# Attention ahead of a mixture of experts: value products of two query halves in two column groups, two pairs behind their scores

## The chip, the cores and the metric

The kernel runs on one NeuronCore of a Trainium2 chip. The metric is the device time of one execution in microseconds (us). The kernel before took 699.36 us (median of three runs, 698.83 to 700.39). The profile shown here is of one execution of 699.8 us.

## The reference, cut to what matters

```
q, k, v: [8, 8, 576, 64] float32                  # batch, heads, positions, head size
scores = q @ k.T / 8
heads 0-3: keep keys with 0 <= pos_q - pos_k < 32                # "local"
heads 4-7: keep keys with pos_k <= pos_q and equal pos % 32      # "strided"
attn = softmax(scores);  x[b, s, h*64:(h+1)*64] = attn @ v
logits = x @ w_gate;  local_gate = sigmoid(x @ w_local)
for s in order: e = argmax(logits[s]) if s == 0 or local_gate[s] < 0.5 else the e of s-1
out[b, s] = softmax(logits[s])[e] * relu(x[b, s] @ w1[e]) @ w2[e]     # 512 -> 1024 -> 512
```

All arithmetic is float32. On TensorE one float32 matmul appears in the trace as two passes, each with its own weight load: six matmuls give twelve records.

## The kernel before, in words

The kernel has two stages. The first is attention with the gate, some 7 to 160 us of the profile. The second is the experts: tokens are sorted by expert into tiles of 128, gathered from the array `xd` in HBM, multiplied by the expert's two matrices, and scattered to the output (L944, L1067, L1088, L1092). The change is in the first stage and in the routing that sorts the tokens.

**A step.** Attention goes by pairs of heads: 8 batches of 4 pairs, two local and two strided, so 32 pairs, one in each step of the loop at L520. Queries are cut into blocks: a local head has six blocks of 96 queries against 128 keys; a strided head is first reordered so that equal residues stand together, and has three blocks of 108 and two of 126. A pair is worked in two units (`Unit`, g = 0 and 1): three blocks each, or three and two. Each step has, on TensorE:

- **scores** (L361): keys are the stationary operand, queries move, 64 rows of contraction. The two heads of the pair lie in the two row halves of the array. ScalarE takes the exponential out of PSUM into the tile `e` (L365), VectorE multiplies it by the mask (L368).
- **values** (L408) of the pair one step behind: `e` of one block is stationary (96, 108 or 126 columns, all 128 rows of contraction or the block's), and the values with a column of ones move. The moving slice is not 65 columns wide but as wide as the block: `values` takes the neighbouring head's columns too and overwrites them with the next product. VectorE adds 1e-9 to the sums (L416), takes the reciprocal (L418) and scales the rows into the x tile `xl` or `xs` (L419).
- **transposes of x** (L445) of the pair two steps behind; ScalarE copies them into `xT` (L449, L452).
- once per batch, **gates** (L462: four products of 32 columns side by side in four column groups) and **choices** (L478), the logits and VectorE's small steps on them.

The x tiles are stored to `xd` by `store_x`, one transfer for a local group (L427), five for a strided one (L431). There is one buffer each of `xl` and `xs`. Loads of q, k and v of the next batch are issued at the first pair of each group (`load`), on the same SyncE queue as the stores. That queue issues in program order: behind a store that waits for VectorE, the next load waits too.

**Order.** The tile framework schedules instructions and keeps each engine's queue in order; `tc.issue_after(x)` forces an instruction behind x on its engine. Before the change only a few places use it.

**Routing.** `route` is a generator that does the bookkeeping of the sort; it runs once for the first three batches (`first`, inside the attention loop, one piece per step), and once for all eight during the first experts. In its pieces stand long VectorE instructions over 576 positions (L580, L587, L668 to L685) and small matmuls. `PIECES` (L69) says at which steps the weights of the first two experts are loaded, eight loads of 1 MB; L228 says where gathers start. At the end of attention the first expert's hidden products fill waits (`filling`, L1067).

Of the kernel before, what the change touches and what calls it, by code (L numbers as in the profile page):

```python
# [19 lines left out]
P = 128  # L20
# [16 lines left out]
SX = 7 * SP  # L37
KW = STRIDE + S
# [3 lines left out]
GC = 32  # L42

# [12 lines left out]
BE = 3  # L56
# [12 lines left out]
PIECES = (7, 9, 11, 13, 15, 16, 17, 18)  # L69
# [3 lines left out]
SUM_LO, SUM_HI = 0.1, 1.0e30  # L73
# [17 lines left out]
class Unit:  # L91


    def __init__(self, b, pair, g):
        self.b, self.pair, self.g = b, pair, g
        self.grp, self.i2 = divmod(pair, 2)
        self.local = self.grp == 0
        self.n = (b * PAIRS + pair) * 2 + g
        if self.local:
            self.w, self.kb, self.m, self.t0 = LQ, LK, 3, 3 * g  # L100
            self.cols = [t * LQ for t in range(3 * g, 3 * g + 3)]
        else:
            self.t0, self.m = (0, 3) if g == 0 else (3, 2)
            self.w = self.kb = SBLK[self.t0][1] * SP
            self.cols = [SBLK[t][0] * SP for t in range(self.t0, self.t0 + self.m)]
# [15 lines left out]
def attention_then_scomoe(ctx: ExitStack, tc: tile.TileContext, q, k, vl, vs, wg, w1, w2, out):  # L121
# [7 lines left out]
    sums = once.tile([P, B * PAIRS * 2, 2, 3], F32, name="sums")  # L129
    nc.gpsimd.memset(sums, 1.0)  # L130
# [3 lines left out]
    passes(tc, False, q, k, vl, vs, wg, w1, w2, views, xd, c, sums, bad)  # L134
    again = nc.values_load(bad[0:1, 0:1], min_val=0, max_val=P,
                           skip_runtime_bounds_check_because="a count of partitions")
    with tc.If(again > 0):

        seen = once.tile([1, 2], F32, name="seen")
        for i, v in enumerate(views):  # L140
            nc.gpsimd.dma_start(out=seen[:, i:i + 1], in_=v[0:1, 0:1])
        nc.gpsimd.tensor_copy(seen, seen)
        passes(tc, True, q, k, vl, vs, wg, w1, w2, views, xd, c, sums, bad)
# [56 lines left out]
def passes(tc, careful, q, k, vl, vs, wg, w1, w2, views, xd, c, sums, bad):  # L200
    with ExitStack() as ctx:
# [8 lines left out]
        with ExitStack() as part:  # L210
# [6 lines left out]
            for n, ins in attention(part, tc, careful, psX, psS, fill, q, k, vl, vs, wg, xd, c, codes, sums):  # L217
                n -= PAIRS * BE + 3

                if n == 0 or n >= 3:  # L220
                    with tc.issue_after(ins):
                        next(first, None)
                if n == PAIRS * (B - BE) - 3:
                    ex.banks = psX
                    ex.turn_x(0)
                if n in PIECES:
                    pieces.pop(0)()
                if 10 <= n < 10 + AHEAD:  # L228
                    ex.gather(n - 10)
            ex.turn_x(1)  # L230
        with ExitStack() as part:
# [3 lines left out]
                     lambda: None if careful else bounds(tc, rp, ex.banks, sums, bad))  # L235
# [4 lines left out]
def bounds(tc, pool, psr, sums, bad):  # L240

    nc = tc.nc
    flat = sums.rearrange("p u h i -> p (u h i)")
    ok = pool.tile([P, B * PAIRS * 12], F32, name="ok")
    nc.vector.tensor_scalar(ok, flat, SUM_LO, None, Alu.is_ge)
    nc.vector.scalar_tensor_tensor(ok, flat, SUM_HI, ok, Alu.is_le, Alu.mult)
# [9 lines left out]
def attention(ctx, tc, careful, psX, psS, fill, q, k, vl, vs, wg, xd, cc, codes, sums):  # L256
# [6 lines left out]
    work = ctx.enter_context(tc.tile_pool(name="work", bufs=4))  # L263
    rows = ctx.enter_context(tc.tile_pool(name="rows", bufs=1))
    small = ctx.enter_context(tc.tile_pool(name="small", bufs=3))
    psV = ctx.enter_context(tc.tile_pool(name="psV", bufs=2, space=PSUM))
# [11 lines left out]
    maskS = consts.tile([SX, SX], F32, name="maskS")  # L278
    nc.gpsimd.memset(maskS, 1.0)
    nc.gpsimd.affine_select(out=maskS, in_=maskS, compare_op=Alu.is_ge, fill=0.0, base=0,  # L280
                            pattern=[[1, SX]], channel_multiplier=-1)
    nc.gpsimd.affine_select(out=maskS, in_=maskS, compare_op=Alu.is_ge, fill=0.0, base=0,
                            pattern=[[-SP, SX // SP], [0, SP]], channel_multiplier=1)
    if careful:
# [8 lines left out]
        addS = consts.tile([SX, SX], F32, name="addS")  # L293
        nc.gpsimd.memset(addS, 0.0)
        nc.gpsimd.affine_select(out=addS, in_=addS, compare_op=Alu.is_ge, fill=NEG, base=0,
                                pattern=[[-1, SX]], channel_multiplier=1)
        nc.gpsimd.affine_select(out=addS, in_=addS, compare_op=Alu.is_ge, fill=NEG, base=SP - 1,
                                pattern=[[SP, SX // SP], [0, SP]], channel_multiplier=-1)
# [25 lines left out]
    st = {}  # L324

    def load(b, grp):
        hs = slice(2 * grp, 2 * grp + 2)
        qt = inp.tile([P, 2, S], F32, name="qt")
        kt = inp.tile([P, 2, KW], F32, name="kt")
        st["q", b, grp], st["k", b, grp] = qt, kt  # L330
        vt = st["v", b, grp] = inp.tile([LK, 2, LT, VW] if grp == 0 else [P, 2, len(SBLK), VW], F32,
                                        name="vst" if grp else "vlt", bufs=2)
        src = (vs if grp else vl)[b]
        if b:
            nc.sync.dma_start(out=qt, in_=q[b][:, hs])
            nc.sync.dma_start(out=kt, in_=k[b][:, hs])
            nc.sync.dma_start(out=vt, in_=src)


        def keys(i2):  # L340
            hq, hk = LT // 2 * LQ, LT // 2 * LQ + STRIDE
            first = grp == i2 == 0
            for c, d in (((slice(0, hq), slice(0, hk)), (slice(hq, S), slice(hk, KW))) if first else
                         ((slice(0, S), slice(0, KW)),)):
                nc.sync.dma_start(out=qt[:, i2, c], in_=q[b][:, hs][:, i2, c])
                (nc.scalar if first else nc.sync).dma_start(out=kt[:, i2, d], in_=k[b][:, hs][:, i2, d])

        return keys, lambda i2: nc.sync.dma_start(out=vt[:, i2], in_=src[:, i2])
# [4 lines left out]
    def scores(u):  # L353
# [4 lines left out]
        for i, c in enumerate(u.cols):  # L358
            for h in range(2):
                r = slice(h * DH, (h + 1) * DH)  # L360
                st["pe"] = nc.tensor.matmul(ps[0:kb, h, i * w:(i + 1) * w], lhsT=kt[r, u.i2, c:c + kb],  # L361
                                            rhs=qt[r, u.i2, c:c + w], start=True, stop=True)
# [3 lines left out]
        mask = maskL if u.local else maskS[0:kb, 0:w]  # L366
        mask = mask.rearrange("x (a b i) -> x a b i", a=1, b=1).to_broadcast([kb, 2, m, w])
        nc.vector.tensor_tensor(blocks(ev, m), blocks(ev, m), mask, op=Alu.mult)  # L368

    def scores_shifted(u):  # L370
# [4 lines left out]
        for i, c in enumerate(u.cols):  # L375
            for h in range(2):
                r = slice(h * DH, (h + 1) * DH)
                nc.tensor.matmul(ps[0:w, h, i * kb:(i + 1) * kb], lhsT=qt[r, u.i2, c:c + w],
                                 rhs=kt[r, u.i2, c:c + kb], start=True, stop=True)
# [3 lines left out]
        for h in range(2):  # L383
            add = addL[:, u.g:u.g + m] if u.local else across(addS[0:w, 0:kb], [w, m, kb])
# [7 lines left out]
        for h in range(2):  # L392
            for i in range(m):
                st["pe"] = nc.tensor.transpose(pt[0:kb, h, i * w:(i + 1) * w], e[0:w, h, i * kb:(i + 1) * kb],
                                               ident[0:w, 0:w])
        nc.scalar.copy(out=u.e[0:kb, :, 0:m * w], in_=pt[0:kb, :, 0:m * w])

    def values(u):
# [3 lines left out]
        vt, pad = st["v", u.b, u.grp], u.w - V1  # L402
        ps = psV.tile([P, 512], F32, name="vps")
        for h, order in ((0, reversed(range(m))), (1, range(m))):
            for i in order:
                o = (h * m + i) * V1 + (pad if h else 0)
                c = 0 if h else VW - w
                st["end"] = nc.tensor.matmul(ps[0:w, o:o + w], lhsT=u.e[0:kb, h, i * w:(i + 1) * w],  # L408
                                             rhs=vt[0:kb, u.i2, u.t0 + i, c:c + w], start=True, stop=True)
# [819 lines left out]
```

## Time and profile before

| what | value |
|---|---|
| time, median of 3 | 699.36 us |
| TensorE matmul busy | 672.7 us, 96% |
| weight loads busy | 577.7 us, 83% |
| VectorE busy | 402.0 us, 57% |
| ScalarE busy | 193.4 us, 28% |
| GpSimd busy | 109.3 us, 16% |
| value products L408 in the chain that ended last | 9% of the span |
| scores L361 in it | 5% |
| transposes L445 in it | 2% |
| expert products L944 in it | 48% |
| HBM traffic over the span | 256 GB/s |

The page of the profile gives busy times and the chain of work that ended last, followed back from the last instruction. A PE row in it with "x24" is 24 passes; the us ahead of it are what they took of the path. The records of single matmuls overlap, so their "mean ns" is a latency and not what one adds to the path: what a pass adds is the distance from start to start. A table by stages gives for each stretch of time the busy us of each engine, with the number of instructions, the granted TensorE clock, the share of the DMA engines' time, and GB/s.

### The profile page before, as it was taken

The page shows a single profiled execution, that of the slowest core. Times are in us where ns is not written, and L with a number is a line of the kernel's source. Part 1 is how long each engine was busy: PE and PEld are TensorE (multiplying, and loading weights), DVE is VectorE, ACT ScalarE, POOL GpSimd, SP SyncE. Part 2 cuts the span into 40 slices and gives each one's busy share as a digit, 9 for nine tenths or more (in the row PEclk, how much of TensorE's full clock was granted, in tenths as well). Part 3 has the DMA queues.
Part 4 walks back from the last instruction along what each step waited for, and adds up shares of the span by engine and source line. Part 5 has one row for each costly group of instructions (what it writes and reads, how often), then busy time and mean ns, then how long its engine had stood idle before and what let it go on. Part 6 is the DMA issues. An engine that isn't in the chain of part 4 may idle for free.

```text
span 699.8 us, 13283 instructions
## 1 busy us (share of the span) xinstructions
PE 672.7 (96%) x5258; PEld 577.7 (83%) x5258; DVE 402.0 (57%) x902; ACT 193.4 (28%) x360; POOL 109.3 (16%) x101
## 2 busy tenths in 40 slices
PE   9999999999999999999999999999999999999970
PEld 8999899887677779999399995799999996869960
DVE  7676888674274257576446956187577541205660
ACT  3545534442111123312132221223313311113220
POOL 1000001101003511120213402021141111011210
PEclk9999999999999999999999999999999999999995
DMA  9988789995778997886768766765688758577210
GB/s 327 387 308 300 232 279 331 339 337 178 283 257 298 318 398 261 277 311 213 273 241 308 252 255 243 248 209 188 209 288 300 274 199 303 216 271 272 62 33 5
DMA packets 74203, 179.83 MB, mean 257 GB/s; under 512 B 9742, under 2 KB 19470, under 8 KB 74128
## 3 DMA queue, kind: packets, MB, share of 16 engines
q1 hardware_dynamic: 67440, 157.91, 64.0%
q0 software_dynamic: 6400, 20.63, 8.7%
q8 instruction: 45, 0.74, 0.4%
q10 hardware_dynamic: 288, 0.31, 0.2%
q14 instruction: 30, 0.25, 0.1%
HBM read 159.80 MB, written 19.55 MB: 256 GB/s over the span
## 4 chain that ended last, share of the span: by engine, by line
PE 90%; DVE 3%; DMA 2%; issue 1%; ACT 1%; SPq 0%; POOL 0%; DVEq 0%; POOLq 0%
PE bank L944 48%; PE bank L1092 10%; PE bank L1067 9%; PE vps L408 9%; PE sps L361 5%; PE xps L445 2%; PE bank L1088 2%; DMA w2t<-in_w_dram 2%; PE xps L462 1%; PE xps L478 1%; PE sps L1067 1%; DMA kt<-in_k_dram 1%; DVE e L368 1%; ACT e L365 0%; DVE w2t L926 0%
## 5 line engine op out<-in xcount | busy, mean ns | idle before, releaser
L887 POOL DMA_INDIRECT xg<-xd,gi x42 | 57.0, 1357 | 301.2 <-PE bank L944 128.7
L1100 POOL DMA_INDIRECT out_dram<-y,si x38 | 49.1, 1292 | 269.3 <-DVE y L1012 136.5
L1092 PE MATMUL bank<-w2t,hT 128*128 128x512 f32 x160 | 70.4, 593 | 0.0
L1067 PEld LDWEIGHTS bank<-xgT,w1t 128*128 128x128 f32 x576 | 65.4, 192 | 2.0 <-issue 1.7
L1067 PE MATMUL bank<-xgT,w1t 128*128 128x128 f32 x576 | 66.2, 276 | 0.0
L1092 PEld LDWEIGHTS bank<-w2t,hT 128*128 128x128 f32 x160 | 29.6, 190 | 33.6 <-issue 33.5
L979 DVE TENSOR_TENSOR part<-bank,part 128x512 f32<-128x512 f32 x13 | 9.0, 693 | 80.3 <-ACT part L976 80.3
L944 PE MATMUL bank<-xs,t 128*128 128x128 f32 x416 | 50.7, 275 | 0.0
L944 PE MATMUL bank<-t,hs 128*128 128x256 f32 x208 | 49.2, 379 | 0.1
L944 PEld LDWEIGHTS bank<-xs,t 128*128 128x128 f32 x416 | 48.5, 192 | 0.0
L944 PEld LDWEIGHTS bank<-xT,w1t 128*128 128x128 f32 x384 | 45.7, 192 | 2.6 <-issue 2.1
L944 PE MATMUL bank<-xT,w1t 128*128 128x128 f32 x384 | 47.4, 276 | 0.0
L969 DVE TENSOR_TENSOR h<-bank,part 128x512 f32<-128x512 f32 x39 | 27.0, 692 | 34.6 <-ACT part L981 22.9
L944 PE MATMUL bank<-xs,w1t 128*128 128x128 f32 x384 | 46.8, 275 | 0.0
L361 PE MATMUL sps<-qt,kt 64*128 64x96 f32 (+2 forms) x704 | 45.9, 275 | 0.6 <-issue 0.4
L944 PE MATMUL bank<-w2t,h 128*128 128x256 f32 x192 | 45.4, 379 | 0.0
L944 PE MATMUL bank<-w2t,hs 128*128 128x256 f32 x192 | 45.4, 379 | 0.0
L361 PEld LDWEIGHTS sps<-qt,kt 64*128 64x128 f32 (+2 forms) x704 | 40.2, 183 | 5.7 <-issue 3.3
L944 PEld LDWEIGHTS bank<-xs,w1t 128*128 128x128 f32 x384 | 44.8, 192 | 0.0
L365 ACT ACTIVATE e<-sps 128x576 f32<-128x576 f32 (+1 forms) x64 | 40.1, 652 | 15.4 <-PE sps L361 11.7
L944 PEld LDWEIGHTS bank<-t,hs 128*128 128x128 f32 x208 | 39.4, 190 | 5.8 <-issue 0.5
L1009 ACT ACTIVATE part<-bank,pt 128x256 f32<-128x256 f32 x39 | 18.6, 476 | 92.2 <-PE bank L944 92.2
(283 smaller groups left out, 1122.9 us busy)
## 6 DMA issues: line engine op xcount, KB each, us to landing
w1t<-in_w_dram SPq DMA_DIRECT2D x50, 1024.0 KB
w2t<-in_w_dram SPq DMA_DIRECT2D x50, 1024.0 KB
kt<-in_k_dram SPq DMA_DIRECT2D x14, 608.0 KB
qt<-in_q_dram SPq DMA_DIRECT2D x14, 576.0 KB
w1x<-in_w_dram SPq DMA_DIRECT2D x6, 1024.0 KB
w2x<-in_w_dram SPq DMA_DIRECT2D x6, 1024.0 KB
vlt<-in_vl_dram SPq DMA_DIRECT2D x7, 780.0 KB
xd<-xl SPq DMA_DIRECT2D x8, 576.0 KB
```

The lines of the kernel that those rows point to most:

```text
L361: st["pe"] = nc.tensor.matmul(ps[0:kb, h, i * w:(i + 1) * w], lhsT=kt[r, u.i2, c:c + kb], rhs=qt[r, u.i2, c:c + w], start=True, stop=True)
L365: nc.scalar.activation(ev, ps[0:kb, :, 0:m * w], Act.Exp, bias=0.0, scale=1.0 / DH ** 0.5)
L408: st["end"] = nc.tensor.matmul(ps[0:w, o:o + w], lhsT=u.e[0:kb, h, i * w:(i + 1) * w], rhs=vt[0:kb, u.i2, u.t0 + i, c:c + w], start=True, ...
L445: st["end"] = nc.tensor.transpose(ps[:, i * w:(i + 1) * w], src[0:w, t, i2 * P:(i2 + 1) * P], ident[0:w, 0:w])
L887: self.nc.gpsimd.indirect_dma_start(out=u["xg"][:, a] if "pair" in u else u["xg"], out_offset=None, in_=self.xd[0:u["rows"]], in_offset=ba ...
L944: self.end = fn(*args, **kw).ins
L969: nc.vector.tensor_tensor(to, ps, add, op=Alu.add)
L1009: nc.scalar.activation(to, ps, Act.Copy, scale=g[r])
L1067: ins = nc.tensor.matmul(ps[:, i * P:(i + 1) * P], lhsT=w1[:, kk, c], rhs=xT[:, kk * P:(kk + 1) * P], start=(kk == 0), stop=(kk == DK - 1))
L1088: ins = nc.tensor.matmul(ps[s], lhsT=hT[:, kk, s], rhs=w[:, kk, :], start=(kk == 0), stop=(kk == FK - 1))
L1092: ins = nc.tensor.matmul(ps, lhsT=hT[:, kk], rhs=w2[:, kk, :], start=(kk == 0), stop=(kk == FK - 1))
L1100: self.nc.gpsimd.indirect_dma_start(out=self.views[0], in_=y, in_offset=None, bounds_check=N - 1, oob_is_err=False, out_offset=bass.Indire ...
```

## The change

What it is for: the value products move as many columns as the block is wide, though only 65 are wanted, and use the array for one product at a time. The change cuts each block of queries in two halves of 48, 54 or 63. The halves stand side by side in two column groups of 64 columns, and write to PSUM partitions 0 and 64 and up. Only the 65 wanted columns move. The rows of x then lie in two halves on partitions 0 to 47 (53, 62) and 64 to 111 (117, 126); the transposes take 112, 118 or 127 rows at once.

```diff
-        for h, order in ((0, reversed(range(m))), (1, range(m))):
-            for i in order:
-                o = (h * m + i) * V1 + (pad if h else 0)
-                c = 0 if h else VW - w
-                st["end"] = nc.tensor.matmul(ps[0:w, o:o + w], lhsT=u.e[0:kb, h, i * w:(i + 1) * w],
-                                             rhs=vt[0:kb, u.i2, u.t0 + i, c:c + w], start=True, stop=True)
+        for h in range(2):
+            for i in range(m):
+                e = u.e[0:kb, h, i * w:(i + 1) * w]
+                e = e.rearrange("x (s p) -> x s p", s=2)
+                for s in range(2):
+                    pe(nc.tensor.matmul, pv[s * HALF:s * HALF + w // 2, h, i], lhsT=e[:, s],
+                       rhs=vt[0:kb, u.i2, u.t0 + i, h * V1:(h + 1) * V1], start=True, stop=True)
...
-        nc.vector.tensor_scalar(rv, pv[:, :, :, DH], 1e-9, None, Alu.add)
-        rc = small.tile([P, 2, 3], F32, name="rc")
-        nc.vector.reciprocal(out=rc[0:w, :, 0:m], in_=rv)
+        dve(nc.vector.reciprocal, out=rv, in_=pv[:, :, :, DH])
```

The 1e-9 is dropped, and a check at the end looks at reciprocals instead of sums. For the halves of a strided block to be halves of the sequence, the order within a strided block becomes position-major; so its mask now depends on the block size (two masks, made in a few more instructions at the start), and its store has two transfers per block, ten in all, with rows of 1 KB as before. A local store becomes two transfers. The ScalarE copy of a strided transpose becomes two copies, one for each half.

The order becomes fixed: `pe` and `dve` chain every TensorE product, and the masks and scalings on VectorE, with `issue_after`. Values come two steps behind their scores, transposes three, gates four; `e` has six buffers instead of four. The order in a step is: scores of pair n, [gates], values of pair n-2 first unit, [choices], values second unit, transposes of pair n-3.

```diff
-    for n in range(len(pairs) + 3):
+    for n in range(len(pairs) + 6):
...
-            if u.i2 == 0 and u.b + 1 < B:
-                load(u.b + 1, u.grp)
+            (load_qk, load_v)[pair % 2](b + (pair != 1), (0, 1, 1, 0)[pair])
...
-        if 0 <= n - 1 < len(pairs):
-            values(pairs[n - 1][0])
+        for g in range(2):
+            if n < len(pairs) and not careful:
+                mask_out(pairs[n][g])
+            if 0 <= n - 2 < len(pairs):
+                values(pairs[n - 2][g])
```

Loads of a next batch are spread over its four pairs. The first routing goes in 22 small pieces instead of one long piece per step, up to two pieces in a step, from step 17 on; two copies of it move from VectorE to ScalarE, and one conversion is folded into a scan. The weights of the first two experts are loaded at steps 25 to 34 instead of 22 to 33, and gathers start at step 29 instead of 25. The second routing keeps its grouping. Nothing in the expert stage is changed, but for where the buffer `y` is placed.

## Prediction

> **What bounds the kernel now.** I read the page's busy row first (PE 672.7 of 699.8 us), then the chain that ended last, then that chain in order of time, then a table of the attention by batches. The page's chain says that TensorE sets the end:
>
> ```profile
> PE 90%; DVE 3%; DMA 2%; issue 1%; ACT 1%; SPq 0%; POOL 0%; DVEq 0%; POOLq 0%
> ```
>
> The chain in order of time, cut to one batch of attention (start, us, what):
>
> ```profile
> 33.19 1.21 PE sps L361 x20
> 34.40 2.21 PE vps L408 x20
> 36.61 0.50 PE xps L445 x6
> 37.11 1.51 PE sps L361 x24
> 38.62 2.21 PE vps L408 x20
> 40.83 0.50 PE xps L445 x5
> 41.33 1.51 PE sps L361 x24
> 42.84 2.21 PE vps L408 x24
> 45.05 0.50 PE xps L445 x5
> 45.55 1.21 PE sps L361 x20
> 46.75 1.11 PE xps L462 x16
> 47.86 1.19 PE vps L408 x12
> 49.05 0.95 PE xps L478 x12
> 50.00 1.09 PE vps L408 x12
> 51.09 0.50 PE xps L445 x6
> ```
>
> No other engine stands in it: a batch is PE work end to end, and half of it (2.21 x 3 + 1.19 + 1.09 = 8.91 of 18.4 us) is value products. The table by stages, one row a batch (PE, PEld, DVE, ACT, POOL busy; clock; DMA share; GB/s), shows where that is not so:
>
> ```profile
> 51.59:69.98 18.39, 18.39 (x228) 16.72 (x228) 13.13 (x46) 9.42 (x20) 0.00 (x0) 1.00 0.87 295
> 69.98:90.95 20.97, 20.01 (x245) 17.91 (x244) 17.75 (x58) 9.42 (x20) 0.00 (x0) 1.00 0.76 247
> 90.95:111.81 20.86, 20.71 (x245) 18.57 (x244) 18.70 (x72) 9.18 (x19) 0.00 (x0) 1.00 0.86 281
> 111.81:132.71 20.90, 19.85 (x246) 17.43 (x246) 13.65 (x52) 9.46 (x21) 3.99 (x4) 1.00 0.97 336
> ```
>
> The three batches that hold the first routing take 20.9 instead of 18.4 us, 7.6 us in all. PE was idle for 0.96 + 0.15 + 1.05 = 2.2 of it; 5.4 is the routing's own matmuls and what they delay. After attention the experts are a second PE-bound stretch, which starts with L576 at 169.66 us. The edits leave it alone, so time won before it should reach the end one to one.
>
> **What a pass costs.** Read from starts of single instructions in the trace. A pass of 96 columns with 96 columns of weights follows the last by 85 ns, of 108 by 95, of 126 by 110. The chain's choices, with 9 moving columns and 96 of weights, go at 0.95 / 12 = 79 ns, so weights alone cost about 0.83 ns a column. The L1092 passes of 512 columns, 6.87 us for 16, cost 429 ns, so streaming costs 0.84 ns a column. A pass thus costs the larger of the two plus some 5 ns. Side by side: the mixed units already run two column groups of 64 with 512 columns. This is the row of the chain:
>
> ```profile
> 342.70 7.09 PE bank L1088 x32
> ```
>
> 222 ns per pass, so 443 for the two, against 429 for one alone: the second is nearly free. In the trace the two start 7 ns apart, then 422 ns to the next two. The two row halves of the scores do the same (7 ns apart, then 105).
>
> **What the Trainium skill says.** "TensorE: Matmul & The Clock Gate", section "LDWEIGHTS (loading the stationary operand)": time goes by columns, P / 1.2 ns; 96 columns give 80, and the trace has 79. The same page, "Part 3: Packing small matmuls", says that tiles at different columns run concurrently, with three of 32 columns 2.38 times as fast; the trace agrees with two of 64 (858 / 443 = 1.94). "TensorEngine Tiling (Array Packing)", "Key Properties": changing the tiling mode drains TensorE. The trace agrees: from transposes to scores 199 ns pass instead of 111, from scores to values 209 instead of 112, from gates to values 356 instead of 242. So a change costs 90 to 115 ns, and the first weight load afterwards shows too (160 instead of 85 ns to the second pass).
>
> **The change part by part, per batch.**
> *Values.* A half-pass streams 65 columns, 54 ns, and loads 48 to 63 columns of weights, 40 to 52 ns. Two halves abreast should follow the last two by 54 + 5 = 59 ns. A local pair has 12 products of two passes, so 24 intervals of 59 = 1.42 us; a strided pair has 20, 1.18 us. Entering the column mode costs 97 ns of drain and some 38 of first load, 0.135. Sum 2 x 1.55 + 2 x 1.315 = 5.73 us, against 4 x 2.21 = 8.84: **-3.11**.
> *Transposes.* The values and the transposes had one mode and now have two: +0.15 each step (97 drain, 50 load). They take 112, 118 or 127 rows instead of 96, 108 or 126: a pass of 96 costs 82 ns, so 6 x 13 more, 0.08, for a local pair, 0.02 for a strided one. 4 x 0.15 + 0.2: **+0.78**.
> *Choices* now stand between column-mode values: two more changes, 0.17 + 0.14: **+0.31**. Scores and gates are as before.
> Together -2.0, so a batch of 18.4 becomes 16.35; eight batches **-16.4 us**.
> *Routing.* Its matmuls stay, in more places, and most get a mode change of their own: about eight times 0.15, +1.2. The idle 2.2 us should shrink, since pieces are short and values have two pairs of slack; but VectorE gets tight (below), so I keep 1.5 of it: **+0.5**. The end of attention waits 0.8 us for a scaling (L419) that will be done in time: **-0.6**.
> *The start.* Scores of pairs 0, 1 and 2 now run ahead of the first values, so the third pair is wanted at 8.7 instead of 10.8 us. By the chain the second pair's k landed at 6.95 us, with 1.2 MB moved by the sizes on the page; the third needs 1.0 MB more, at the 392 GB/s of the first full batch 9.6 us. Pair 4 needs 5.2 MB in all, at 17.1 us, where PE could start it at 15.8. **+2.2**.
> *Transfers later.* The seven batches of that table from 14.8 to 151.1 us sum to 42.9 MB; the same in 121 us is 354 GB/s. The best batch had 392 at a share of 1.02, so it just fits. The worst place is where weights, the last q, k, v and stores meet (share 0.97 to 0.98 in the last two batches): 8 MB of weights, 6.2 of q, k, v and stores and 0.8 of gathers in ten steps of 3.9 us. There VectorE already waited once 2.0 us for a store of `xl`. The x tiles still have one buffer each, and the store's lead is two shorter steps. Behind such a wait stand, on VectorE, the next mask and scaling, and behind these TensorE's values, as the two value banks are not free. Allowed: **+1.5**.
> *Cost nothing:* the dropped VectorE addition (0.15 us a unit on an engine that isn't the bound), the reciprocal from PSUM, and masks made at the start (some 2 us more VectorE setup, which ended at 5.1 us, before the first values at 9.9). The ten strided store issues take 0.7 us each of SyncE today, so at most 7 of some 16 us. Split ScalarE copies: 728 and 650 ns for 324 and 252 columns today, 78 ns apart for 72 columns, so up to 0.38 us of each is fixed; four copies instead of two then add 0.75 us a strided pair, at worst 3.4 us of ScalarE in a 3.4 us step, without a wait as the scores have two buffers. At best, with the slope alone, they are cheaper than now.
> Sum: -16.4 + 0.5 - 0.6 + 2.2 + 1.5 = -12.8: **686.5 us**.
>
> **Rivals.**
> 1. *Transfers or VectorE take over (27%).* For: the sums above. If 341 GB/s, the rate of the last full batch, is all that can be sustained, 42.9 MB take 125.7 us instead of 121, another 4.7 us, 691. VectorE had 17.75 and 18.70 us of work in the two routing batches, where TensorE would now need about 18; if it misses as it did before, 2 to 3 us more, up to 694. Against: 392 GB/s was reached, and two pairs of slack absorb a late mask.
> 2. *Small halves do not overlap (10%).* All side-by-side evidence has 288 or 512 moving columns, or row halves. If the loads of one half shut out the streaming of the other, each half-pass costs 59 ns by itself, 88 x 59 = 5.2 us more a batch: 8 x 5.2 = 42 us, 686.5 + 42 = 728, **slower than before**. If only a fixed cost per instruction shows and an interval is 85 ns, the change is 704 x 26 = 18 us short of its aim: 705. Against: row halves of 96 columns keep 7 ns distances, and four instructions fit in 59 ns.
> 3. *A new wait each batch (5%).* Gates need ScalarE's copies of the transposes just done, stores delay loads: half a us in each of 32 steps is 16 us, 702, also slower.
>
> **How the numbers follow.** Side by side as computed 58% (681 to 690), rival 1 27% (690 to 695), rival 2 10%, rival 3 5%. The interval counts 704 times: 54 ns would give 3.5 us back, 70 take 7.7. Mode changes, 48 more, bounded at 0.09 and 0.18 us each, move it by -2.7 or +1.6. The start and the transfers, 3.7 us, can be 0 or double. The lower end takes interval and start at their good ends; the upper end takes rival 1 whole: 681 to 695. Slower: rivals 2 and 3, less the chance that they are mild, 12%. Faster 86%, same 2%.
>
> **What would show it.** The chain should give value rows of about 1.5 (x48) and 1.3 us (x40), transposes of 0.65 to 0.75, and a quiet batch of 16.3 us; the last routing's first matmuls (L576, at 169.66 us) should start near 157. Value rows of 2 us or more mean rival 2. Batches of 17 us or more with DMA, DVE or ACT rows in the chain mean rival 1 or 3. A different length of the expert stage would mean that the one-to-one step was wrong.

## The result, and the profile after

The changed kernel takes 706.84 us (median of four runs, 706.32 to 708.80), beside 699.10 us for the kernel before: 1.0113 times as long (95% interval 1.0089 to 1.0136). The prediction was 686.5 us with a range of 681 to 695, and 12% for slower. It was wrong by 20 us and in its sign. Of the four executions of e15 below, the one that lay 1.7% above the fastest, at a lower clock, is left out.

The profiled execution takes 705.1 us. First the shares of the chain of waits that ended last, then a stretch of that chain in order of time (start, us, what), with one whole batch and what follows it:

```profile
PE 81%; DMA 10%; DVE 4%; SPq 2%; issue 1%; POOL 0%; DVEq 0%; ACT 0%; POOLq 0%; ACTq 0%
```

```profile
38.12 1.51 PE sps L361 x24
39.63 1.28 PE vps L361 x40
40.92 0.72 PE xps L361 x6
...
46.31 1.50 PE vps L361 x48
47.81 0.68 PE xps L361 x5
48.49 1.21 PE sps L361 x20
49.70 1.11 PE xps L361 x16
50.80 0.82 PE vps L361 x24
51.62 1.12 PE xps L361 x12
52.74 0.82 PE vps L361 x24
...
59.08 11.51 DMA vst<-in_vs_dram
70.58 0.02 issue
70.60 0.75 SPq L493
...
74.28 6.33 DMA kt<-in_k_dram
```

(All of TensorE's products in attention now go through one helper, so they stand under its line, L361; the tile tells them apart.) The first part is what was predicted, row by row: values of 1.50 and 1.28 us, transposes of 0.67 to 0.72, choices of 1.12. The batch takes 16.16 us. Then the chain leaves TensorE: a load of v is 11.5 us on the path, four issues of stores (L493) follow, and then a load of k. Before, 90% of the chain was TensorE and 2% transfers.

The table by stages of the changed kernel: the start, the first three stretches of a batch each, and one late stretch (PE, PEld, DVE, ACT, POOL busy; clock; DMA share; GB/s):

```profile
0.00:18.76 18.76, 13.31 (x208) 12.35 (x209) 14.48 (x57) 6.96 (x11) 3.98 (x24) 1.00 0.92 336
18.76:38.12 19.36, 19.36 (x316) 16.97 (x316) 11.24 (x27) 8.38 (x21) 0.00 (x0) 0.82 0.67 239
38.12:54.28 16.16, 16.16 (x316) 14.04 (x316) 12.21 (x38) 8.92 (x24) 0.00 (x0) 1.00 0.81 272
54.28:74.28 20.00, 18.59 (x363) 16.23 (x364) 12.99 (x39) 10.80 (x28) 0.00 (x0) 1.00 0.77 261
137.43:161.94 24.51, 15.06 (x247) 12.40 (x247) 10.57 (x32) 6.43 (x19) 4.63 (x5) 0.93 0.81 291
```

The third row is the only batch without a loss. In the second row TensorE is busy throughout and still takes 3.2 us more: its clock is 0.82. In the last row it idles for 9.5 of 24.5 us. Behind the start the memory is not at its limit: 239 to 291 GB/s at 67 to 81% of the DMA engines' time, where the kernel before had 392 GB/s in one batch.

**Where the time went.** The last routing's first matmuls (L576 before, L639 after) start at 169.66 us before and at 176.87 after, 7.2 us later. The two rows of the chains, then the table by stages up to there, before and after:

```profile
169.66 1.18 PE bank L576 x12
```

```profile
176.87 1.18 PE bank L639 x12
```

```profile
0.00:169.66 169.66, 164.79 (x1948) 149.48 (x1949) 121.97 (x439) 78.00 (x155) 8.20 (x26) 1.00 0.87 300
```

```profile
0.00:176.87 176.87, 154.31 (x2653) 133.90 (x2653) 116.32 (x386) 75.13 (x189) 9.11 (x29) 0.96 0.81 281
```

From there to the last scatter both take 510.8 us. So all of the loss is in attention. TensorE's busy time ahead of that point falls from 164.8 to 154.3 us, and its idle time rises from 4.9 to 22.6. The trace's clock records explain the rest: three stretches of 6.8, 3.4 and 3.4 us at half clock, each just behind a wait of 2.8 to 4.9 us, cost 6.8 us. Without them TensorE's work would have shrunk by some 17 us, close to the predicted 16.4. The change won what it was said to win, and lost 18 us to waits and some 7 to the clock.

**What SyncE does.** The order of SyncE's queue (start, us of issuing, what), first of the kernel before, then of the changed one:

```profile
40.86 0.33 SPq L337 DMA_DIRECT2D vst<-in_vs_dram  x1
41.28 4.00 SPq L431 DMA_DIRECT2D xd<-xs  x5
45.38 0.84 SPq L335 DMA_DIRECT2D qt<-in_q_dram  x1
```

```profile
46.72 7.88 SPq L493 DMA_DIRECT2D xd<-xs  x10
54.70 0.40 SPq L380 DMA_DIRECT2D qt<-in_q_dram  x1
55.15 0.82 SPq L381 DMA_DIRECT2D kt<-in_k_dram  x1
56.01 0.43 SPq L386 DMA_DIRECT2D vlt<-in_vl_dram  x1
56.54 1.17 SPq L488 DMA_DIRECT2D xd<-xl  x2
```

The ten strided stores hold SyncE for 8 us, half a batch, with no load among them. In 28.67 to 36.90 us, the first such burst, the table by stages gives 126 GB/s, in 46.72 to 54.70 it gives 189; the kernel before had 307 and 298 in its bursts of five. SyncE's waits (for whom: us, times, longest), from 20 to 170 us, before and after:

```profile
SPq L337 <- PE xps L445: 26.4, 8, 5.9
```

```profile
SPq L380 <- PE sps L361: 6.8, 3, 6.4
SPq L493 <- DMA vst<-in_vs_dram: 5.7, 5, 1.9
SPq L493 <- DMA kt<-in_k_dram: 4.2, 4, 1.7
```

Before, the loads waited for TensorE to free a buffer: they were early. After, that wait is nearly gone, and the stores wait for landings of other transfers. The instructions in the trace show why: every transfer issued by SyncE or ScalarE counts up one of eight semaphores (counters on which engines wait) in turn, and is held until the transfer that had that one last has landed. Of these transfers a batch had 13 before and has 19 now.

### The profile page after: what moved, and what is told of

Read it like the earlier page. It is cut to its first block, busy times and chain, and to the rows that moved or that the text cites. A ratio compares the mean times of both kernels' runs of the same rounds, so it can differ in the third digit from the quotient of the medians.

```text
span 705.1 us, 14706 instructions
## 1 busy us (share of the span) xinstructions
PE 662.0 (94%) x5962; PEld 562.7 (80%) x5962; DVE 394.6 (56%) x846; ACT 190.9 (27%) x396; POOL 107.5 (15%) x104
## 4 chain that ended last, share of the span: by engine, by line
PE 81%; DMA 10%; DVE 4%; SPq 2%; issue 1%; POOL 0%; DVEq 0%; ACT 0%; POOLq 0%; ACTq 0%
PE bank L1020 47%; PE bank L1168 10%; PE bank L1143 9%; DMA w2t<-in_w_dram 4%; PE vps L361 4%; DMA kt<-in_k_dram 3%; PE xps L361 3%; PE sps L361 3%; PE bank L1164 2%; DMA vst<-in_vs_dram 2%; PE sps L1143 1%; DMA vlt<-in_vl_dram 1%; SPq L493 1%; DMA xd<-xs 1%; DVE e L366 1%
## 5 line engine op out<-in xcount | busy, mean ns | idle before, releaser
L963 POOL DMA_INDIRECT xg<-xd,gi x42 | 53.4, 1271 | 300.6 <-DVE inv L366 129.5
L361 PE MATMUL sps<-qt,kt 64*128 64x96 f32 (+2 forms) x704 | 47.2, 281 | 4.1 <-DMA kt<-in_k_dram 4.0
L361 PEld LDWEIGHTS sps<-qt,kt 64*128 64x128 f32 (+2 forms) x704 | 41.6, 188 | 9.2 <-issue 5.5
```

What stands on the lines that cost most here:

```text
L361: st["pe"] = product(*args, **kw).ins
L963: self.nc.gpsimd.indirect_dma_start(out=u["xg"][:, a] if "pair" in u else u["xg"], out_offset=None, in_=self.xd[0:u["rows"]], in_offset=ba ...
```

## The experiments

Each is timed in three rounds beside the kernel before on the same chip. "Last routing" is the start of that routing's first matmuls in the profiled execution (before 169.66, after 176.87 us). That is one execution, and those of one kernel lie 1 us (e11) to 13 us (e9) apart, so a few us between two last routings decide nothing. "Closing" is the time from the last scatter's issue to the end (before 19.3, after 17.4 us), which turned out not to be constant. The expectations count the runs by their e-numbers.

### A. The stores leave SyncE

All x stores by GpSimd, and then half of them:

```diff
-                nc.sync.dma_start(out=dst[h], in_=src[...])
+                nc.gpsimd.dma_start(out=dst[h], in_=src[...])              # e1, also the strided ones
+                (nc.gpsimd if h else nc.sync).dma_start(out=dst[h], ...)   # e6
```

> The changed kernel with the stores of x issued by GpSimd instead of SyncE; same bytes, same shapes, everything is computed. Theory A (SyncE queue: the ten strided store issues of 0.75 us and its eight completion slots hold back the loads behind them): the DMA rows of k and v between 54 and 157 us leave the chain, only the start's 10 us of waiting for k stay; batches near 16.5 us, 684 to 692 us. Theory B (bandwidth: the bytes of a batch do not fit in a 16 us batch): the loads stay late, 703 to 708 us. Theory C (one buffer of xs: VectorE waits for the store to land and TensorE with it): the stores land no earlier, 698 to 706 us.

> The changed kernel, with one of the two halves of every x store issued by GpSimd, so that SyncE issues five strided stores a batch as before the change, and GpSimd the other five. Everything is computed. Theory (issue time on SyncE): SyncE is back at some 4 us of strided stores a batch, so most of the 13 us that all ten on GpSimd brought come back: 693 to 698 us. Rival (a store that waits for VectorE stands in SyncE's order ahead of the loads, however few the stores are): the first half-store still stands there with the same wait, so little is gained: 702 to 707 us.

Measured: e1 693.72 us, 0.9916 of before (0.9884 to 0.9948), last routing at 160.40. e6 683.41 us, 0.9734 (0.9682 to 0.9786), last routing at 162.80, closing 12.5 us. In e6 SyncE's wait for a free buffer is back, and two batches running are quiet (SyncE's waits, then the table by stages):

```profile
SPq L380 <- PE sps L361: 26.6, 6, 6.0
```

```profile
37.77:53.94 16.17, 16.17 (x317) 14.05 (x316) 12.17 (x38) 8.94 (x24) 3.42 (x6) 1.00 0.93 321
53.94:70.10 16.16, 16.16 (x316) 14.03 (x316) 12.15 (x38) 8.93 (x24) 3.42 (x6) 1.00 0.90 305
```

The stores on SyncE are what cost the gain: taking all or half away brings 16.5 or 14.1 us of attention. A half-store that still stands there, waiting for VectorE, does little harm. e1 fell between the ranges of theories A and C, and e6 was 10 us faster than either of its ranges; what isn't attention in its lead is its closing (part F) and the spread of its executions, 678 to 688 us. What these two runs leave together is SyncE's time and the number of transfers that share the eight semaphores: both fell.

### B. The stores alone, in the kernel before

```diff
-                nc.sync.dma_start(out=dst[c:c + n], in_=src[0:n * SP, t])
+                m = (n + 1) // 2
+                nc.sync.dma_start(out=dst[c:c + m], in_=src[0:m * SP, t])
+                nc.sync.dma_start(out=dst[c + m:c + n], in_=src[m * SP:n * SP, t])
```

> The kernel before, with only its stores cut in two as the change cuts them: two transfers instead of one for a local group, ten instead of five for a strided group, the same bytes to the same places. Everything is computed. Theory (issue time): a strided store takes SyncE 0.70 to 0.75 us to issue, so five more a batch take 3.6 us more of SyncE, 29 us over eight batches; but a batch lasts 18.4 us here and not 16.2, so part of it fits: I expect 700 to 706 us, with rows of k, v or x transfers in the chain of waits that were not there. Rival (the steps became too short for the memory, the stores have nothing to do with it): no change, 698.5 to 700.5 us and a chain that is TensorE end to end.

Measured: 719.1 us, 1.0276 (1.0249 to 1.0303), last routing at 186.19. The chain of this kernel, early in attention, where before has only TensorE:

```profile
34.76 8.50 DMA vst<-in_vs_dram
43.25 0.02 issue
43.27 8.89 DMA xd<-xs
52.16 0.02 issue
52.17 6.79 DMA xd<-xs
```

Cutting the stores in two, with nothing else changed, costs 19 us even where a batch has 18.4 us; 6.8 us of it are two stretches of 6.8 us at half clock behind waits. The theory's sign was right and its size (to 706) too small. These stores run on fewer DMA engines still than the changed kernel's (see the last section), so the 19 us aren't to be carried over as they are.

### C. Rivals: late issue of loads, the one x tile, the burst

e2 issues the loads of q, k and v from the second batch on by ScalarE; e3 gives back the early load order of before; e9 has two buffers of the strided x tile (in the first pass only: e4, which had them also in the rerun that the program keeps for numbers out of range, gave no time, as there was no room for them); e7 the same with all stores on GpSimd; e12 leaves ten stores on SyncE but issues five of them one step later, behind that step's loads.

```diff
-            nc.sync.dma_start(out=st["k", b, grp], in_=k[b][:, hs])
+            nc.scalar.dma_start(out=st["k", b, grp], in_=k[b][:, hs])   # e2, q and v too
-            (load_qk, load_v)[pair % 2](b + (pair != 1), (0, 1, 1, 0)[pair])
+            if pair % 2 == 0:                                           # e3
+                load_qk(b + 1, pair // 2)
+                load_v(b + 1, pair // 2)
-                                   rows.tile([...], F32, name="xs"))
+                                   rows.tile([...], F32, name="xs", bufs=1 if careful else 2))  # e9, e7
-                store_x(u.b, u.grp)
+                store_x(u.b, u.grp, (0,) if u.grp else (0, 1))          # e12
+            if n >= 3 and pairs[n - 3][1].pair == PAIRS - 1:
+                store_x(pairs[n - 3][1].b, 1, (1,))
```

> The changed kernel with the loads of q, k and v from the second batch on issued by ScalarE instead of SyncE; stores stay on SyncE. Everything is computed. Theory A: loads no longer stand behind stores, most of the loss comes back, 685 to 694 us; the stores may still be late by their own 7.5 us of issue. Theory B: no change, 703 to 708 us. Theory C: the loads' rows leave the chain, but rows of the store of xs and of VectorE take their place, 696 to 704 us.

> The changed kernel with the loads of q, k and v of a group all issued at the group's first pair, as in the kernel before, instead of spread over four pairs. Everything is computed. Theory A: v gets one or three more steps of lead, k and q none, and all still stand behind the stores: a part comes back, 696 to 704 us. Theory B: no change or slower by queueing, 703 to 709 us. Theory D (the spread loads alone are the cause): all comes back, 684 to 692 us.

> The changed kernel with all stores on SyncE as it has them, and two buffers of the strided x tile instead of one. Everything is computed. Theory (the ten store issues, 8 us in one piece, hold the loads back): the stores still take 8 us of SyncE in one piece, so little is won: 703 to 708 us. Rival (what hurts is that VectorE waits for the x tile until its stores have landed): that wait, 4.8 us in 3 times and what hangs on it, is gone: 694 to 700 us.

> All x stores issued by GpSimd, as in the first experiment, and two buffers of the strided x tile instead of one, so that VectorE can scale into the next batch's tile before the stores of this one have landed. Everything is computed. Theory (what is left there is the wait of VectorE for landed stores: 3.4 us in 4 waits, of which 2.7 us reach TensorE, but the chain of waits puts 7% of the span on stores): 2 to 5 us less than the 693.7 us of the first experiment, so 689 to 692 us, with no wait of the scaling for a strided store. Rival (what is left is the number of transfers and the memory's rate): as the first experiment, 693 to 694.5 us.

> The changed kernel with all stores on SyncE and the same ten strided stores a batch, but in two groups: five when the strided pairs are done, the other five one step (some 4 us) later, behind that step's loads. Everything is computed. Theory (the harm is one piece of 8 us in which only 54 KB transfers start, one each 0.75 us, and no load): two pieces of 4 us with loads between them: 690 to 699 us. Rival (the sum of issue time or the number of transfers per batch is the limit, wherever they stand): 704 to 709 us; and if the later landing makes VectorE wait for the tile, it shows in its waits for strided stores, with 700 us or more.

| run | us | ratio to before (interval) | last routing |
|---|---|---|---|
| e2 | 719.57 | 1.0247 (1.0185 to 1.0310) | 187.65 |
| e3 | 706.35 | 1.0076 (1.0056 to 1.0097) | 172.56 |
| e9 | 702.97 | 1.0048 (1.0031 to 1.0064) | 169.80 |
| e7 | 688.69 | 0.9839 (0.9808 to 0.9869) | 156.52 |
| e12 | 702.37 | 1.0055 (1.0037 to 1.0074) | 171.80 |

Neither the order of the loads nor the tile is the main cause: e3 and e9 stay above before. The tile is a part of it: e9 stands at 1.0048 of before, the changed kernel at 1.0113, some 4 us. e2 made it worse, above all of its ranges: ScalarE then waits for landings ahead of its own work, once for 11.7 us until a `qt` had landed. With the stores away the tile is worth 5 us: e7's last routing is at 156.5 us, where the prediction had 157. e12 refutes the theory as I had it, that the harm is one piece of 8 us: in two pieces of 4 it gave 4.5 us back, not 8 to 17, which lies between its ranges. A sum per batch, of time or of transfers, was left.

### D. Time or number of the stores

e13 issues half of the stores by ScalarE, which shares the eight semaphores. e17 and e18 keep SyncE and the place in its order, and send the strided group as twelve transfers of 48 rows, or six of 96, to rows that follow one another. In these two the strided heads' rows lie in the wrong places, at the same amount of work.

```diff
+                    (nc.scalar if h else nc.sync).dma_start(...)               # e13
+            for t in range(LT):                                                # e17
+                for h in range(2):
+                    r = (2 * t + h) * m                                        # m = 48
+                    nc.sync.dma_start(out=dst[r:r + m], in_=src[h * HALF:h * HALF + m, min(t, len(SBLK) - 1)])
+            for t in range(LT):                                                # e18
+                nc.sync.dma_start(out=dst[t * LQ:t * LQ + LQ], in_=src[0:LQ, min(t, len(SBLK) - 1)])
```

> The changed kernel, with one half of every x store issued by ScalarE, where the sixth experiment has GpSimd. Everything is computed. Theory (SyncE's time): the last routing's first product starts near 163 to 167 us as with GpSimd (162.8), plus what ScalarE's own waits cost, and the end is 18 us long as in the changed kernel: 690 to 696 us. Rival (the few outstanding transfers that SyncE and ScalarE share are the limit): it starts at 171 us or later, 699 us or more.

> The changed kernel with all stores on SyncE, but each batch's ten strided stores of 54 or 63 rows replaced by twelve of 48 rows to rows that follow one another: the same bytes in more transfers, of a shape that SyncE should issue in the 0.33 to 0.5 us of the local stores. The rows of the strided heads land in the wrong places, so the experts work on other numbers; the amount of work is the same. Theory (the shape: 0.75 us each, few DMA engines): SyncE needs 4 to 6 us a batch for them, the last routing starts at 158 to 166 us, and with the long end of 18 us the time is 687 to 696 us. Rival (the number of transfers in the queue, or their order): it starts at 175 us or later, 704 us or more.

> As the seventeenth experiment, but the same 576 rows go in six transfers of 96 rows instead of twelve of 48, at the same place in SyncE's order. As there, the strided heads' rows land in the wrong places, and the amount of work is the same. Theory (number of transfers: each one waits for the one eight before it to land, so many small ones keep the loads behind them waiting): SyncE is through with them in 3 us instead of 6 to 7.8, the last routing starts at 157 to 166 us instead of 179.5, and with the closing work of 17 to 19 us the time is 686 to 695 us. Rival (the order: whatever stands behind a store that waits for VectorE comes late): the place is the same, so the last routing starts at 174 us or later and the time is 702 us or more.

Measured: e13 724.29 us, 1.0346 (1.0283 to 1.0408), last routing at 189.12. That is in the rival's range, but doesn't decide: ScalarE's copies waited 24.3 us for stores to land. e17 705.33 us, 1.0091 (1.0059 to 1.0122), last routing at 179.47. e18 696.04 us, 0.9925 (0.9905 to 0.9944), last routing at 165.55. SyncE's queue in e17, then in e18:

```profile
46.10 7.36 SPq L494 DMA_DIRECT2D xd<-xs  x12
```

```profile
28.81 3.50 SPq L492 DMA_DIRECT2D xd<-xs  x6
```

A store of 48 rows takes SyncE 0.42 us in most cases, not 0.75, and twelve of them still hold it for 7.4 us here, as some of the issues wait for an earlier landing. SyncE's waits in e17, then one in e18:

```profile
SPq L494 <- DMA vst<-in_vs_dram: 8.1, 5, 2.4
SPq L494 <- DMA kt<-in_k_dram: 7.1, 4, 2.6
```

```profile
SPq L488 <- DVE xl L366: 17.6, 7, 4.2
```

Half the number, at the same bytes, engine and place, brings 14 us of attention in the profiled executions, and 12 us of time by the ratios to before. So the number of transfers in SyncE's queue is what costs, and a cheaper issue alone doesn't cure it. The issues of the strided stores, their number times what most of them take, sum to 60 us of SyncE in the changed kernel, 40 in e17 and 21 in e18; SyncE's waits for landings, from 20 to 170 us, to 16, 32 and 8 us. What e17 won on the issues it lost to the waits, while fewer transfers cut both. Which of the two weighs more in the changed kernel isn't separated: no run has the same number of transfers at another price, or the same issue time under another limit.

The order isn't the main cause, but not cleared either. e18 came in a us above the range given, its last routing is 9 us behind e7's, and its later batches still take 18 to 20 us. In it SyncE waits 17.6 us for VectorE ahead of local stores, with loads behind them. Whether that is the rest stays open.

### E. The start

The first loads in the order in which scores two pairs ahead need them, and the second batch's first group pair by pair (e8: with e1's stores; e10: with e6's stores and two `xs`):

```diff
-        for pair in range(PAIRS + 1):
+        for pair in range(PAIRS + 2):              # q and k of pairs 0 to 5, the last two of batch 1
...
-            if pair:
-                grp, i2 = divmod(pair - 1, 2)
+            if pair >= 2:
+                grp, i2 = divmod(pair - 2, 2)      # v two pairs behind
```

> All x stores issued by GpSimd, as in the first experiment, and the first loads put in the order in which scores two pairs ahead of the values need them: q and k of each pair ahead of the values of the pair two behind, and the first two pairs of the second batch loaded pair by pair instead of as one group. Everything is computed. The fifth pair then needs about 4.0 MB instead of 5.2 MB ahead of it. Theory (the start is bound by the bytes that must land first): the scores of pair 4 start at 15.8 to 17 us instead of 18.7, TensorE idles 2 to 3 us less in the first 19 us, and the time falls by 1 to 2.5 us below the 693.7 of the first experiment: 691 to 692.7 us. Rival (the wait at the start is made up later, since other transfers then stand in the way): 693 to 694.5 us.

> Three things together: one half of every x store issued by GpSimd (683.4 us by itself), two buffers of the strided x tile (5 us less when all stores were on GpSimd), and the first loads in the order of need (0.8 us less there). Everything is computed. If the parts add up: 678 to 682 us. If the one tile was a limit only when all stores came late by GpSimd: 682 to 684.5 us.

Measured: e8 692.85 us, 0.9895 (0.9855 to 0.9935), last routing at 163.32, so no earlier than e1: nothing that the spread of these runs lets one tell. e10 682.00 us, 0.9746 (0.9721 to 0.9771), last routing at 158.93, the fastest of all. Its first batch's logits are copied at 33.0 us, in e6 at 36.3; that part of the start is worth some 3 us where the stores don't stand in the way. It accounts for most of the 3.9 us by which e10's last routing is ahead of e6's, so a second tile is worth little there; 682.0 us lies on the border of both ranges and doesn't tell.

### F. The end of the kernel

e11 moves two of five strided stores of the kernel before to GpSimd. e14 adds sixteen loads of four bytes to that engine, nothing else. e15 and e16 are e10 with other stores on GpSimd: all strided ones, or both local ones and half of the strided.

```diff
+                (nc.gpsimd if t % 2 else nc.sync).dma_start(out=dst[c:c + n], in_=src[0:n * SP, t])  # e11
+        if n == 6:                                                                                     # e14
+            for i in range(16):
+                nc.gpsimd.dma_start(out=more[:, i:i + 1], in_=wg[0:1, i:i + 1])
```

> The kernel before, with two of the five strided stores of a batch issued by GpSimd instead of SyncE. Everything is computed. Theory: the kernel before is bound by TensorE and its five issues, 4 us of 18.4, hold nothing back, so nothing is to be won: 698.5 to 700.5 us, and the whole of what the changed kernel gains from the same step is the cure of a new trouble. Rival (moving stores off SyncE helps either kernel): 690 to 697 us.

> The kernel before, with sixteen loads of four bytes each issued by GpSimd in the middle of attention, which nothing reads. Everything is computed. If GpSimd's closing work goes by the number of transfers it has issued (80 there, 96 here and in the eleventh experiment): it takes some 10 instead of 19 us after the last scatter, and the time is 690 to 692 us with the attention as before. If the closing work was shorter there because the stores were moved: 698.5 to 700 us.

> The changed kernel with all ten strided stores of a batch on GpSimd, the local ones on SyncE, two buffers of the strided x tile and the first loads in the order of need. Everything is computed. Theory (it is the strided stores' 0.75 us each that hold the loads back, the local ones take 0.33 to 0.5): the last routing starts at 154 to 158 us; GpSimd issues 160 transfers, whose closing work I can't compute from the counts seen (80: 19 us, 96: 10, 128: 12, 176: 18): 676 to 687 us. Rival (local stores hold loads back as well): it starts at 160 us or later.

> The changed kernel with both local stores and five of the ten strided ones on GpSimd, two buffers of the strided x tile and the first loads in the order of need. Everything is computed. Theory: as the tenth experiment (682.0 us, last routing at 158.9), less the wait of one batch in which a local store landed late, 3 to 5 us: it starts at 154 to 158 us. GpSimd issues 136 transfers; the time is 676 to 687 us for the same reason. Rival (that batch is long because of the weights' loads): 158 to 160 us.

| run | us | ratio to before (interval) | last routing | GpSimd transfers | closing |
|---|---|---|---|---|---|
| e11 | 691.31 | 0.9888 (0.9870 to 0.9906) | 168.26 | 96 | 10.0 |
| e14 | 703.59 | 1.0030 (1.0019 to 1.0041) | 172.05 | 96 | 19.8 |
| e15 | 690.91 | 0.9809 (0.9761 to 0.9857) | 167.14 | 160 | 13.9 |
| e16 | 685.46 | 0.9757 (0.9722 to 0.9791) | 158.37 | 136 | 13.7 |

e11 is faster than before by 7.7 us, in the rival's range, but for another reason: only 1.4 us are in attention. The others are behind the last scatter. The last row of the chain, of before and of e11:

```profile
679.41 1.01 POOL out_dram L1100
```

```profile
679.11 1.01 POOL out_dram L1100
```

The scatters stand at the same time, and the spans are 699.8 and 690.1 us. In those 10 to 20 us GpSimd does closing work, of which one drain and two counter instructions vary: the drain takes 6.6 us in before and after, 6.0 in e1 and e7, 3.3 in e15 and e16, 2.0 in e6 and e10, 1.05 in e11 and 7.9 in e14. It is the same in every kernel with the same set of GpSimd's transfers. But it doesn't go by their number: 96 give the shortest and the longest. What it does go by stays open. For the comparison of attention, e7 is the fair one, as its closing (17.8 us) is as long as that of before: 0.9839. e15 goes against the theory that only strided stores matter, and the number in SyncE's queue, nine a batch, doesn't explain it either: the last routing came at 167 us, VectorE waited 5.2 us for a local store to land, and TensorE ran 20 us at half clock. Why the local stores landed so late there wasn't tried further. With both of them on GpSimd, e16, the last routing came at 158.4 us, just outside the 154 to 158 expected and no earlier than in e10; its time was in the range.

## Why the prediction was wrong, point by point

*Values, transposes, choices, batch.* Right. Values 1.50 and 1.28 us for 1.55 and 1.315, transposes 0.67 to 0.72 for 0.65 to 0.75, choices 1.12 for 0.95 + 0.17, a quiet batch 16.16 us for 16.35. Two halves in two column groups do overlap (rival 2 is out): two abreast follow the last two by 57 ns in the trace, for 59. TensorE's work in attention fell by 16.6 us in e7, and by some 18 without its one stretch at half clock, for 16.4. Three slips of the working don't matter here: the passes of the choices start 85 ns apart in the trace, not 79, as those do that move 96 columns; the transposes' terms sum to 0.80, not 0.78; and eight times 2.02 us is 16.2.

*The expert stage.* Right: 510.8 us from the last routing to the last scatter in both, so what attention wins or loses goes to the end one to one.

*"Cost nothing: ... The ten strided store issues take 0.7 us each of SyncE today, so at most 7 of some 16 us."* **This is the step that failed.** The price was nearly right, 0.75 us each and 7.9 to 8.2 us in all. What it left out is who is queued behind: the loads of the next batch, behind stores that fill SyncE's time and its eight semaphores, which now pass 19 transfers a batch instead of 13. The edit was held against the time that SyncE has in a batch, and its cost lies in the loads that it holds back. Undone in three ways (e1, e6, e18) it gives back 11 to 16.5 us of attention; made alone in the kernel before (e5) it costs 19 us.

*"Transfers later: +1.5."* Mis-sized by the same oversight. The working compared bytes with the memory's rate: 354 GB/s needed, 392 seen. With the stores elsewhere the rate was there: e7 has 326 GB/s over all of attention up to the last routing, and gets there at 156.5 us. That this lies half a us from the 157 of the prediction is in part luck: e7 too started later than forecast, with its 3.4 us of half clock behind a wait there, and its TensorE work shrank by more. With them on SyncE it was 281. The row of e7:

```profile
0.00:156.52 156.52, 148.15 (x2652) 129.24 (x2653) 116.50 (x386) 75.04 (x189) 64.52 (x125) 0.99 0.93 326
```

In the changed kernel TensorE's idle time behind the fifth pair's start grew by 14 us (3.2 to 17.1), not 1.5, and half clock behind such waits took 3.4 us more.

*The start, +2.2.* Too small. The fifth pair's scores were forecast for 17.1 us and came at 18.76. Up to them TensorE idled for 5.4 us (18.76 - 13.31), and for 1.7 in the kernel before, so +3.8:

```profile
0.00:14.80 14.80, 13.12 (x142) 12.44 (x142) 10.81 (x44) 5.30 (x8) 3.26 (x21) 1.00 0.89 310
```

A second term was missing: after the wait TensorE ran 6.8 us at half clock, another 3.4 us.

*Rivals.* "Stores delay loads", in rival 3 at 5% and 702 us, is what happened, at 706.8. It deserved its own line in the change's sum, with the number of transfers before and after. Rival 1 named VectorE and the memory's rate, and e7, which has the same VectorE work and moves the bytes in less time, shows that neither was the bound.

## What to carry to other kernels

When an edit splits a transfer, count the transfers in that queue for each stage before and after, and ask what is queued behind them; the issuing engine's busy time and the mean GB/s can both look fine. The sign to look for is in the issuing engine's own waits: in the kernel before and in e6 its loads waited 26 us for a buffer to come free, so there was slack; in the changed kernel that wait was down to 7 us, and the stores waited for landings. Stores that can't be merged can go to another queue, as in e1 and e7, but look at the kernel's end as well before the gain is credited to the stage.

## What the runs showed of the hardware that was not expected

- A store's rows are not always spread over all DMA engines. A strided store of 54 or 63 rows raised its semaphore in ten steps: one at 1.2 us, nine as data landed; those of before in seven or eight, those of e5 in four or five, the loads in sixteen. The Trainium skill's "DMA: Bandwidth & Descriptors", section "Why a DMA increments its semaphore by 16 and not by 1", says so: a transfer uses as many engines as the largest number up to 16 that divides the outermost size on both of its sides (here 9, 6 or 7, 3 or 4); each of them adds one, and the issuing sequencer writes the rest at once. The steps agree. Such a store mostly takes 0.75 us to issue in the changed kernel, and one of 48 rows 0.31 to 0.42 in e17.
- Short waits can cost TensorE more than their length. Waits of 1.2 to 6.5 us were often followed by 3.4, 6.8 or 10.2 us at half clock: in e6 one of 1.3 us at 109 us by 10.2, which made that batch 23.9 us from gates to gates, against 19.6 in e7. Not always: e1 waited four times for 1.0 to 2.3 us in attention and kept the full clock, and e14 had 3.4 us of half clock without a wait of 0.8 us or more ahead of it. The multiples of 3.4 agree with the window that "TensorE: Matmul & The Clock Gate" states in its Part 1; but it speaks of an idle window, and here shorter waits came before the half clock.
- "Perfetto Trace Analysis", section "DMA Optimizations", says that split transfers may let some start sooner, for DMA engines that are generally idle. Here they were busy for 87% of attention's time in the kernel before, and splitting the stores cost 19 us (e5). Another point of that section, to give loads and stores different issuing engines, is what helped (e1, e6, e7).
- The length of GpSimd's closing drain, 1.05 to 7.9 us, changes with the set of transfers that GpSimd has issued, by a law that these runs don't show.
